# A gated mix of a long convolution and a mixer MLP: W1 products of one block ahead of the convolution taps, eight more steps and four evacuation engines changed, and ring slots given to the buffer that was free the longest

## The chip, the cores and the metric

The kernel runs on 1 core of one Trainium2 chip. The time is device microseconds of one execution. Three runs of the kernel before are at hand; one further execution was recorded by the hardware profiler, and all rows of a trace come from that one. A time within a row is counted from the first instruction of the span.

The engines are named as in the profile: PE is TensorE (PEld its weight loads), DVE is VectorE, ACT is ScalarE, POOL is GpSimd, and SP is the engine that issues most DMAs.

## The reference

S is 2048 tokens, D is 640, F is 1536, all inputs bf16. Cut to what matters (padding of the shifts and casts left out):

```python
g = sigmoid((q * gate_w).sum(-1, keepdims=True))

kv = short_conv(k, shift_k) * v                  # 4 taps along the tokens
y  = causal_long_conv(kv, ssm_k) + kv * ssm_D    # by rfft2/irfft2 of length 4096
a  = q * y

h  = gelu(layernorm(q) @ w1)                     # D x D
hs = shifted(h) @ w2                             # four groups of columns, shifted by +1, -1, +2, -2 tokens
x1 = q + hs
b  = x1 + gelu(layernorm(x1) @ w3) @ w4          # D x F, F x D

out = g * a + (1 - g) * b
```

## The kernel before, in words

Partition p holds 16 consecutive tokens (index t), so the sequence is handled in four blocks (0 to 3) of 4 x 128 tokens. All matrix products run on PE into eight PSUM banks; ACT and DVE empty the banks; SP starts the DMAs.

The work around the change is this:

- `k_load(c)` (L556) loads a block of k and turns it with PE (`transposed`, L610: 20 transposes into three PSUM banks `pst`), and copies each bank into `KT`. The letters of the step name say which engine empties which bank (`evac`, L358: ACT on L360, DVE on L362).
- `x_stats`, `x_norm`, `x_turn` give the layer norm of a block of q (held in `X`) and turn the result `xn` into `xt`. For blocks 0 and 1 the turn is made by PE and three copies; for blocks 2 and 3 (`D`) it is one DMA transpose that SP issues (L652).
- `mlp1(c, u)` (L700) makes the W1 products of block c, group u (five matmuls into a bank `psm1`, L707), and in a second step the GELU of that bank on ACT (L710) into `HT`.
- `tap(k, ev)` (L577) makes the four-tap convolution for 128 channels with matmuls of 32 x 128 (L590) into four banks `psk`, and multiplies with v: for an A the bank is first copied to `yk` on ACT (L599) and then multiplied on DVE (L602), for a V it is multiplied on DVE straight from the bank (L605).
- `t2_table` (L306) makes a table of twiddle factors in two halves: DVE makes integers `ab` (L266), POOL adds them into a grid `n` (L321), DVE masks it (L275), and ACT takes the sine. Its step 3 adds 2048 to `ab` for the second half.
- `step1` (L410) is the first stage of the transforms: matmuls into banks `ps1` (L423), and casts into `stg`, whose engine is given by a letter for each bank. `w2` (L777) makes the W2 products (L788), which DVE adds to X (L791).
- `w3` (L840) makes the W3 products and the GELU (L844) into ring buffers `gt`, and `w4` (L867) multiplies those with W4. `step4` (from L893) makes the last stage of the inverse transform and gates the result.

The order of all work is written out: `ORDER` holds 1099 step names of the form `step.arguments:k`, and the loop at the end calls the k-th piece of each step in that order, under a manual schedule. Each engine's queue is therefore exactly what the steps give it in that order, and an engine waits in order. The buffers of seven rings are also written out: `SLOTS` (L66) has one digit for each allocation of a tag, and `slot` (L81) takes them one after the other. Tag `c` are the eight PSUM banks, `row` four buffers of 4 x 640 values (k, xn, stg, q), `gt` four buffers shared by `n`, `ab` and the GELU results, and the others are smaller rings. A buffer is written only when those who read its earlier tenant are done.

```python
def slot(pl, shape, dt, name, tag, bufs):
    if tag not in SLOTS:
        return pl.tile(shape, dt, name=name, tag=tag, bufs=bufs)
    taken[tag] = taken.get(tag, -1) + 1
    return pl.tile(shape, dt, name=name, tag=tag + SLOTS[tag][taken[tag]], bufs=1)
```

Of the kernel before, what the change touches and what calls it, by code (L numbers as in the profile page):

```python
# [41 lines left out]
def kernel(  # L42
# [24 lines left out]
        "c": "012345670124703510347205142356401723605162370514731057423671045261304732641374153670421350627413"  # L67
             "502634751264351270361427503164257364102546173045621537426107432715604371401362570164301257613045"
             "267236057416537621507362651374026372401534762501373150427102547535706432073125640736450750634127"
             "504763270415367204325170635147630125460327156034215760147362304167135620316425031672301402715320"  # L70
             "1724107361761423564023714053627501267420674256271306234",
        "row": "01230213021302320123012031203120310310303",
        "gt": "012301031010231012301201",
# [805 lines left out]
    def step4(t1, ev):  # L879
# [32 lines left out]
        "open.L1.left:0 "  # L912
        "open.A2.right:0 "
        "consts0:0 "
        "load_x0.0:0 "
        "warm:0 "
        "load_x0.1:0 "
        "consts0:1 "
        "warm:1 "
        "warm:2 "  # L920
        "pow0:0 "
        "kv_alloc:0 "
        "k_load.3.AVA:0 "
        "f4_table:0 "
        "x_stats.0.VVVA:0 "
        "warm:3 "
        "k_load.3.AVA:1 "
        "x_stats.0.VVVA:1 "
        "load_x.1:0 "
        "x_stats.0.VVVA:2 "  # L930
        "k_load.3.AVA:5 "
        "x_stats.0.VVVA:3 "
        "x_stats.0.VVVA:4 "
        "x_stats.0.VVVA:5 "
        "x_stats.0.VVVA:6 "
        "warm:4 "
        "row_order:0 "
        "k_load.2.VAV:0 "
        "f1_table:0 "
        "x_norm.0.VVAA:0 "  # L940
        "x_norm.0.VVAA:1 "
        "f4_table:1 "
        "x_stats.1.VVVV:0 "
        "k_load.3.AVA:2 "
        "load_x.3:0 "
        "x_norm.0.VVAA:2 "
        "x_stats.1.VVVV:1 "
        "k_load.3.AVA:3 "
        "x_turn.0.AAA:0 "
        "k_load.3.AVA:6 "  # L950
        "k_load.2.VAV:5 "
        "load_w1.1:0 "
        "x_norm.0.VVAA:3 "
        "k_load.2.VAV:1 "
        "x_stats.1.VVVV:2 "
        "x_turn.0.AAA:1 "
        "x_stats.1.VVVV:3 "
        "x_turn.0.AAA:2 "
        "x_stats.1.VVVV:4 "
        "load_w1.0:0 "  # L960
        "x_stats.1.VVVV:5 "
        "x_stats.3.VVAA:0 "
        "k_load.3.AVA:4 "
        "x_norm.1.VVVV:0 "
        "x_turn.0.AAA:4 "
        "k_load.2.VAV:3 "
        "x_turn.0.AAA:3 "
        "x_turn.0.AAA:5 "
        "x_stats.3.VVAA:1 "
        "x_norm.1.VVVV:1 "  # L970
        "x_norm.1.VVVV:2 "
        "v_load.2:0 "
        "k_load.0.AAV:0 "
        "f1_table:1 "
        "mlp1.0.2:0 "
        "mlp1.0.3:0 "
        "x_norm.1.VVVV:3 "
        "v_load.0:0 "
        "k_load.1.AVV:0 "
        "k_load.2.VAV:6 "  # L980
        "mlp1.0.0:0 "
        "load_x.2:0 "
        "x_stats.3.VVAA:2 "
        "x_turn.1.VVV:0 "
        "x_turn.1.VVV:4 "
        "mlp1.0.1:0 "
        "x_stats.3.VVAA:3 "
        "x_turn.1.VVV:1 "
        "k_load.2.VAV:4 "
        "x_stats.3.VVAA:4 "  # L990
        "x_stats.3.VVAA:5 "
        "k_load.0.AAV:3 "
        "x_turn.1.VVV:5 "
        "mlp1.0.3:1 "
        "x_stats.3.VVAA:6 "
        "x_turn.1.VVV:2 "
        "v_load.3:0 "
        "x_turn.1.VVV:3 "
        "k_load.1.AVV:3 "
        "w1_mixed:0 "  # L1000
        "v_load.1:0 "
        "mlp1.0.0:1 "
        "x_stats.2.VVAA:0 "
        "mlp1.0.2:1 "
        "k_load.0.AAV:1 "
        "mlp1.0.1:1 "
        "x_stats.3.VVAA:7 "
        "k_load.0.AAV:5 "
        "mlp1.1.2:0 "
        "x_norm.3.VVVV:0 "  # L1010
        "x_norm.3.VVVV:1 "
        "k_load.0.AAV:4 "
        "load_cj:0 "
        "k_load.0.AAV:2 "
        "mlp1.1.2:1 "
        "x_norm.3.VVVV:2 "
        "x_norm.3.VVVV:3 "
        "x_stats.2.VVAA:1 "
        "k_load.1.AVV:5 "
        "mlp1.0.4:0 "  # L1020
        "k_load.1.AVV:4 "
        "mlp1.0.4:1 "
        "k_load.1.AVV:1 "
        "d_fold:0 "
        "mlp1.1.4:0 "
        "x_turn.3.D:0 "
        "kv_consts:0 "
        "x_stats.2.VVAA:2 "
        "mlp1.1.0:0 "
        "k_load.2.VAV:2 "  # L1030
        "k_wrap:0 "
        "k_load.1.AVV:6 "
        "mlp1.1.4:1 "
        "k_load.0.AAV:6 "
# [7 lines left out]
        "x_stats.2.VVAA:4 "  # L1042
        "h_shift.1:0 "
        "mlp1.1.3:1 "
        "tap.4.VAAV:0 "
        "x_stats.2.VVAA:5 "
        "tap.3.VAVA:1 "
        "tap.3.VAVA:3 "
        "tap.3.VAVA:5 "
        "h_shift.0:0 "  # L1050
# [1014 lines left out]
```

## Time and profile before

| what | us |
|---|---|
| the runs | 227.49, 231.56, 227.55 |
| median | 227.55 |
| the profiled execution | 227.13 |
| its span, first to last instruction | 225.4 |

The granted TensorE clock is 1.00 in the profiled execution. The difference between 227.13 and 225.4 lies around the span and is no part of any row.

How to read the rows that are shown further on. The line by stretch gives the stretch, its length, the busy time of PE, PEld, DVE, ACT and POOL with the number of instructions in brackets, then the granted clock, the busy share of the DMA engines and GB/s. A row of the chain of waits gives start, length and what ran. A row of the timeline gives start, length, engine, line, operation, output and inputs with shapes and how many were merged (x5); in square brackets stands how long the engine sat idle before it and what released it. A merged row's time to the next row's start is what the engine spent on it; its own length runs to the end of the last instruction, and matmuls overlap. Rows name tiles without their numbers.

### The profile page before, as it was taken

To read this page: it belongs to the slowest core of one execution; us is meant where nothing else is said; L and a number is where in the kernel's file an instruction comes from. 1 tells how busy PE (TensorE), PEld (TensorE's weight loads), DVE (VectorE), ACT (ScalarE), POOL (GpSimd) and SP (SyncE) were. 2 spreads that over 40 slices of the span, in tenths; PEclk is the share of its full clock that TensorE was granted. 3 is DMA by queue.
4 is the path that set the end of the run, shared out by engine and by line. 5 is a ranking of instruction groups with operands and counts; after the bars stand their busy time and mean duration, and the time that the engine had idled before them with its cause. 6 is when DMAs were issued, how large, how long until landed. Compare 5 with 4: busy or idle time off the path is not lost.

```text
span 225.4 us, 6053 instructions
## 1 busy us (share of the span) xinstructions
PE 217.8 (97%) x2427; PEld 121.5 (54%) x2428; DVE 183.7 (81%) x447; ACT 171.4 (76%) x341; POOL 38.1 (17%) x91
## 2 busy tenths in 40 slices
PE   8989999899999999999999999999999999999994
PEld 2557455447846563345664444556533547657762
DVE  7898998868889969963899988989999841439994
ACT  4899988787999999999987597967988450266450
POOL 4247246816000431300600000000000000000000
PEclk9999999999999999999999999999999999999999
DMA  6999998892998999999989570690794879429914
GB/s 226 374 376 344 258 280 170 317 364 107 361 365 355 348 295 265 410 334 343 254 219 338 116 243 0 191 379 17 119 305 166 249 259 366 175 60 305 324 70 179
DMA packets 41770, 57.61 MB, mean 256 GB/s; under 512 B 18446, under 2 KB 34446, under 8 KB 41486
## 3 DMA queue, kind: packets, MB, share of 16 engines
q1 hardware_dynamic: 41166, 54.60, 75.4%
q0 software_dynamic: 576, 2.62, 3.1%
q8 instruction: 19, 0.31, 0.6%
q14 instruction: 9, 0.07, 0.1%
HBM read 34.93 MB, written 18.35 MB: 236 GB/s over the span
## 4 chain that ended last, share of the span: by engine, by line
PE 79%; DMA 9%; DVE 4%; ACT 4%; issue 1%; POOL 1%; SPq 0%; ACTq 0%
PE ps L840 24%; PE ps L867 23%; PE psw L788 7%; PE ps L465 5%; PE ps L893 4%; DMA X<-in_A_q_dram 4%; PE psm L707 4%; DMA xt<-xn 3%; PE psz L228 3%; PE ps L512 3%; PE ps L423 2%; PE pst L390 2%; DVE X L791 2%; ACT stg L360 2%; DMA S_x<-stg 2%; PE psk L590 1%
## 5 line engine op out<-in xcount | busy, mean ns | idle before, releaser
L840 PE MATMUL ps<-x1t,W 128*128 128x512 bf16 x240 | 56.1, 380 | 0.1
L867 PE MATMUL ps<-W,gt 128*128 128x320 bf16 (+2 forms) x383 | 55.1, 299 | 0.1
L867 PEld LDWEIGHTS <-gt 128*128 128x128 bf16 x384 | 36.2, 98 | 17.7 <-issue 3.0
L844 ACT ACTIVATE gt<-ps 128x512 bf16<-128x512 f32 x48 | 27.6, 609 | 19.0 <-PE ps L867 10.6
L840 PEld LDWEIGHTS <-W 128*128 128x128 bf16 x240 | 21.9, 98 | 28.7 <-issue 5.9
L360 ACT CAST stg<-ps 128x512 bf16<-128x512 f32 x55 | 28.6, 604 | 2.3 <-PE ps L423 2.0
L870 DVE SCALAR_TENSOR_TENSOR X<-ps,OMG,X 128x320 bf16<-128x320 f32 (+2 forms) x32 | 17.2, 547 | 11.9 <-PE ps L867 11.7
L707 PE MATMUL psm<-xt,WA 128*128 128x512 bf16 x100 | 23.4, 379 | 1.9 <-DMA WA<-in_B_w_dram 0.8
L360 ACT CAST gs<-ps 128x320 bf16<-128x320 f32 x41 | 15.6, 440 | 8.8 <-PE ps L512 4.8
L788 PE MATMUL psw<-WA,HT 128*128 128x320 bf16 x116 | 21.4, 300 | 0.0
L362 DVE CAST XS<-ps 128x512 bf16<-128x512 f32 x19 | 12.5, 684 | 6.7 <-PE ps L465 6.7
L362 DVE CAST stg<-ps 128x512 bf16<-128x512 f32 x25 | 15.8, 683 | 1.9 <-PE ps L423 1.9
L707 PEld LDWEIGHTS <-WA 128*128 128x128 bf16 x100 | 9.2, 97 | 12.9 <-DMA WA<-in_B_w_dram 1.0
L360 ACT CAST hs<-ps 128x512 bf16<-128x512 f32 x28 | 15.0, 605 | 1.4 <-PE ps L465 1.4
L791 DVE SCALAR_TENSOR_TENSOR X<-psw,X 128x320 bf16<-128x320 f32 x32 | 14.5, 487 | 1.6 <-PE psw L788 1.6
L897 ACT ACTIVATE y<-ps,GS 128x320 bf16<-128x320 f32 x22 | 10.4, 526 | 5.7 <-PE ps L893 3.5
L710 ACT ACTIVATE HT<-psm 128x512 bf16<-128x512 f32 x20 | 11.8, 617 | 3.6 <-PE psm L707 3.5
L788 PEld LDWEIGHTS <-HT 128*128 128x128 bf16 x116 | 10.7, 98 | 6.8 <-issue 3.1
L362 DVE CAST gs<-ps 128x320 bf16<-128x320 f32 x23 | 10.7, 484 | 2.4 <-PE ps L512 1.7
L797 ACT ACTIVATE jk<-X 128x640 bf16<-128x640 bf16 x16 | 12.2, 761 | 0.5 <-DVE X L791 0.4
L788 PE MATMUL psw<-WA,HM 128*128 128x320 bf16 x44 | 12.3, 299 | 0.0
L360 ACT CAST XS<-ps 128x512 bf16<-128x512 f32 x21 | 11.8, 607 | 0.5 <-PE ps L465 0.3
(151 smaller groups left out, 346.6 us busy)
## 6 DMA issues: line engine op xcount, KB each, us to landing
S_x<-stg SPq DMA_DIRECT2D x8, 640.0 KB, 4.3
S_h<-stg SPq DMA_DIRECT2D x8, 640.0 KB, 4.8
ax<-S_x SPq DMA_DIRECT2D x8, 640.0 KB, 5.9
ax<-S_h SPq DMA_DIRECT2D x8, 640.0 KB, 8.1
S_g<-gs SPq DMA_DIRECT2D x8, 640.0 KB, 3.6
W<-in_B_w_dram SPq DMA_DIRECT2D x2, 1920.0 KB, 9.1
kn<-in_A_k_dram SPq DMA_DIRECT2D x4, 640.0 KB, 6.9
E<-in_A_ssm_k_dram SPq DMA_DIRECT2D x5, 512.0 KB, 6.1
```

Source lines behind the costliest of these rows:

```text
L360: A.copy(out=dst, in_=src)
L362: V.tensor_copy(out=dst, in_=src)
L465: PE.matmul(ps[j][q:q + 32, lo - 512 * u:hi - 512 * u], lhsT=CMP[HALF[j], 8 * b + 4 * h + i, c, :], rhs=st[name, 2 * b + h][HALF[j], i, lo ...
L707: PE.matmul(ps[:].rearrange("p (a b) -> p a b", a=4), lhsT=W1N[:, k, 160 * u:160 * u + P] if u < 4 else W1M[:, k, :], rhs=xt[:, :, k, :], ...
L710: A.activation(out=st["HT"][:, 4 * c:4 * c + 4, u, :], in_=ps[:].rearrange("p (t b) -> p t b", t=4), func=ACT.Gelu_apprx_tanh)
L788: PE.matmul(ps[:], lhsT=h_tile(f, t1), rhs=W2P[:, f, o:o + W], start=(f == 0), stop=(f == 4))
L791: V.scalar_tensor_tensor(out=X1[:, t1, o:o + W], in0=box["ps"][:], scalar=1.0, in1=X[:, t1, o:o + W], op0=ALU.mult, op1=ALU.add, accum_out ...
L797: A.activation(out=jk[:], in_=X1[:, t1, :], func=ACT.Square, accum_out=S12[:, 1, t1:t1 + 1])
L840: PE.matmul(ps[:].rearrange("p (a b) -> p a b", a=4), lhsT=st["W3"][:, k, f * P:(f + 1) * P], rhs=xt[:, :, k, :], start=(k == 0), stop=(k ...
L844: A.activation(out=st["gt", c, f // 4][:, f % 4, :], in_=ps[:], func=ACT.Gelu_apprx_tanh)
L867: PE.matmul(ps[:], lhsT=st["gt", c, f // 4][:, f % 4, i * P:(i + 1) * P], rhs=st["W4"][:, f, o:o + w], start=(f == 0), stop=(f == FC - 1))
L870: V.scalar_tensor_tensor(out=X1[:, t1, o:o + w], in0=box["ps"][:], scalar=OMG[:, t1:t1 + 1], in1=X1[:, t1, o:o + w], op0=ALU.mult, op1=ALU ...
```

## The change

The set of steps is the same. Of the 1099 steps these stand elsewhere (place before, place after): `mlp1.1.1:0`, the W1 products of block 1 and group 1, 139 to 127, and its GELU `mlp1.1.1:1` 147 to 135; `k_load.1:2` (the transposes of the second bank) 127 to 112; `load_w2:0` 125 to 138; `tap.3:0` 128 to 133 and `tap.4:0` 133 to 140; `t2_table:3` 443 to 320; `w2.14:3` 447 to 449; `step4.10:2` and `step4.8:6` change places near the end (1078, 1077).

Four evacuations change their engine: the first bank of `k_load.0` (into KT) from ACT to DVE; the third bank of `x_turn.1` (into xt) from DVE to ACT; one bank of `step1.KV.3` and one of `step1.HT0.1` (into stg) from ACT to DVE.

The digits of the rings `c` and `gt` are others. For `c` most of it gives the same sequence of tenants under other numbers. In `gt`, the last half differs in four places.

The diff, cut to its core (the list `ORDER` is also written with several steps to a line, which changes nothing):

```diff
     SLOTS = {
-        "c": "012345670124703510347205142356401723605162370514731057423671045261304732641374153670421350627413"
...
+        "c": "012345670124703513043725174501674235064513206457025460372105436712450347102340263145072365174023"
...
-        "gt": "012301031010231012301201",
+        "gt": "012301031012031201301201",
...
-        "x_stats.2.VVAA:3 "
-        "t2_table:0 "
-        "load_w2:0 "
-        "mlp1.1.3:0 "
-        "k_load.1.AVV:2 "
-        "tap.3.VAVA:0 "
-        "mlp1.1.0:1 "
...
+        "x_stats.2.VVAA:3 t2_table:0 mlp1.1.3:0 mlp1.1.1:0 mlp1.1.0:1 x_stats.2.VVAA:4 h_shift.1:0 mlp1.1.3:1 "
+        "x_stats.2.VVAA:5 tap.3.VAVA:0 tap.3.VAVA:1 mlp1.1.1:1 tap.3.VAVA:3 tap.3.VAVA:5 load_w2:0 h_shift.0:0 "
```

The first place is PE's queue at the end of the W1 products of block 1. `psm1` is a bank of W1 products, `psk` one of the taps. Before:

```order
L707 MATMUL psm1_539<-xt_385,WA_103 128x512
L590 LDWEIGHTS KT_155
L590 MATMUL psk_546<-DG_506,KT_155 128x128
L590 LDWEIGHTS KT_155
L590 MATMUL psk_547<-DG_506,KT_155 128x128
```

And after:

```order
L707 MATMUL psm1_538<-xt_385,WA_103 128x512
L707 LDWEIGHTS WA_103
L707 MATMUL psm1_544<-xt_385,WA_103 128x512
L707 LDWEIGHTS WA_103
L707 MATMUL psm1_544<-xt_385,WA_103 128x512
L707 LDWEIGHTS WA_103
L707 MATMUL psm1_544<-xt_385,WA_103 128x512
L707 LDWEIGHTS WA_103
L707 MATMUL psm1_544<-xt_385,WA_103 128x512
L707 LDWEIGHTS WA_103
L707 MATMUL psm1_544<-xt_385,WA_103 128x512
L590 LDWEIGHTS KT_155
```

The five matmuls of group 1 (psm1_544; before it was psm1_716, behind two taps) now stand ahead of the first tap.

The second place is DVE's queue at the normalisation of block 3 (xn_461), whose end lets SP issue the first DMA transpose. Before:

```order
L664 TENSOR_SCALAR xn_461<-X_102,RS_91,NB_92 128x640 x4
L362 COPY KT_155<-pst_419 128x1024
L552 TENSOR_REDUCE i32_507<-IDB_75 128x32
L553 TENSOR_TENSOR DG_506<-i32_507,cr_465 128x640
L362 COPY KT_155<-pst_269 128x1024
```

And after:

```order
L664 TENSOR_SCALAR xn_461<-X_102,RS_91,NB_92 128x640 x2
L362 COPY KT_155<-pst_438 128x1024
L664 TENSOR_SCALAR xn_461<-X_102,RS_91,NB_92 128x640 x2
L362 COPY KT_155<-pst_419 128x1024
L552 TENSOR_REDUCE i32_508<-IDB_75 128x32
```

The copy of pst_438 stands between the second and the third piece of the normalisation; it was ACT's before.

The third place is DVE's queue at the second half of the twiddle table (ab, n), between the additions of W2 products to X. Before:

```order
L791 SCALAR_TENSOR_TENSOR X_102,S12_82<-psw2_1692,X_102 128x320
L266 TENSOR_SCALAR ab_534<-ab_534 128x32
L275 TENSOR_SCALAR n_1753<-n_1753 128x1024
L341 TENSOR_SCALAR n_1756<-m_1532 128x512
L275 TENSOR_SCALAR n_1756<-n_1756 128x512
L791 SCALAR_TENSOR_TENSOR X_102,S12_82<-psw2_1743,X_102 128x320
```

And after:

```order
L791 SCALAR_TENSOR_TENSOR X_102,S12_82<-psw2_1693,X_102 128x320
L362 CAST stg_1727<-ps1_1721 128x4x128
L275 TENSOR_SCALAR n_1753<-n_1753 128x1024
L341 TENSOR_SCALAR n_1756<-m_1533 128x512
L275 TENSOR_SCALAR n_1756<-n_1756 128x512
L791 SCALAR_TENSOR_TENSOR X_102,S12_82<-psw2_1730,X_102 128x320
```

The addition to ab has left this place for one 123 steps earlier, and a cast of a bank of step 1 stands where it was.

More of the change, by code (lines that the diff above doesn't have):

```diff
@@ L911 @@
     ORDER = (
[L912 to L1034, printed above, removed]
-        "x_stats.2.VVAA:3 "
-        "t2_table:0 "
-        "load_w2:0 "
-        "mlp1.1.3:0 "
-        "k_load.1.AVV:2 "
-        "tap.3.VAVA:0 "
-        "mlp1.1.0:1 "
[L1042 to L1050, printed above, removed]
-        "mlp1.1.1:0 "
@@ L1382 @@
-        "step1.HT0.0.VAAVVAVAVV:4 "
-        "step1.HT0.0.VAAVVAVAVV:6 "
-        "step1.HT0.0.VAAVVAVAVV:1 "
-        "w3.0.9:1 "
-        "swap.L1.L2.left:0 "
-        "step1.HT0.0.VAAVVAVAVV:5 "
-        "step1.HT0.1.VVAAAAAAVA:1 "
-        "w3.0.6:0 "
-        "step1.HT0.1.VVAAAAAAVA:2 "
-        "w2.4:4 "
-        "step1.HT0.0.VAAVVAVAVV:12 "
-        "w3.0.6:1 "
-        "step1.HT0.0.VAAVVAVAVV:7 "
-        "step1.HT0.0.VAAVVAVAVV:8 "
-        "w3.0.7:0 "
-        "step1.HT0.0.VAAVVAVAVV:9 "
@@ L2008 @@
-        "store.8:1 "
-        "close.L2:0 "
-        "close.C:0 "
[169 rows of a table added]
     ).split()
```

948 lines of the change are left out of this document (4 added, 944 removed), and 167 rows, old and new, of the table ORDER.

## The prediction

> **What bounds the kernel now.** I read the page's busy shares first, then the busy time by stretch.
>
> ```profile
> span 225.4 us, 6053 instructions
> PE 217.8 (97%) x2427; PEld 121.5 (54%) x2428; DVE 183.7 (81%) x447; ACT 171.4 (76%) x341; POOL 38.1 (17%) x91
> ```
> ```profile
> 10.00:20.00 10.00, 8.47 (x91) 5.77 (x89) 9.69 (x33) 9.94 (x18) 4.45 (x6) 1.00 1.06 364
> 40.00:50.00 10.00, 9.25 (x124) 3.86 (x108) 7.99 (x15) 7.59 (x16) 5.32 (x9) 1.00 0.90 349
> 90.00:220.00 130.00, 129.94 (x1433) 70.82 (x1434) 103.31 (x196) 92.48 (x195) 5.90 (x18) 1.00 0.72 228
> ```
>
> The first figure behind the length is PE's busy time. From 90 to 220 PE is busy for 129.94 of 130.00 us, so there a delay of another engine matters only if it outlasts PE's cover, and what PE does is unchanged. PE loses time before 20 us, 0.75 in 40 to 50, and a little in 80 to 90. The end is therefore set by the last moment at which PE waits for something outside itself. The chain of waits names it.
>
> ```profile
> 24.32 7.63 DMA xt<-xn
> 39.69 1.12 PE psk L590 x76
> 40.83 0.59 ACT yk L599
> 41.46 2.33 PE psm L707 x10
> ```
> ```profile
> 41.46 1.89 PE L707 MATMUL psm<-xt,WA 128*128 128x512 bf16 x8 [0.75 <-ACT yk L599]
> ```
> ```profile
> 39.14 0.58 ACT L599 CAST yk<-psk 128x512 bf16<-128x512 f32 x1
> ```
> ```profile
> 24.32 4.08 SPq L652 DMA_TRANSPOSE xt<-xn  x1
> 34.74 3.73 SPq L652 DMA_TRANSPOSE xt<-xn  x1
> ```
> ```profile
> DMA to landing us min/median/max: 6.6/7.1/7.6
> ```
>
> PE's 0.75 us before 41.46 is put down to a cast of yk, but the bank that these W1 products of block 2 take was read by the earlier cast, which ended at 39.14 + 0.58 = 39.72. The other input is block 2's turned x: the second DMA transpose is issued at 34.74, and with the shorter landing time of 6.6 it is there at 41.34. I take that transpose as the wait that ends last. Behind 41.46 PE has no wait until 85. So the time goes with the second transpose's issue, less what PE gets back later.
>
> **Term 1: the KT copy on VectorE, +0.61.** The copy of the first bank of k_load.0 goes from ACT to DVE, between the second and third normalisation of x block 3.
>
> ```profile
> 21.78 0.89 DVE L685 BATCH_NORM_STATS2 b<-X 128x6 f32<-128x320 bf16 x2 [0.53 <-DMA X<-in_A_q_dram]
> ...
> 22.82 1.47 DVE L664 TENSOR_SCALAR xn<-X,RS,NB 128x640 bf16<-128x640 bf16 x4
> 24.21 0.68 DVE L362 COPY KT<-pst 128x1024 bf16<-128x1024 bf16 x1
> 24.82 0.36 DVE L552 TENSOR_REDUCE i<-IDB 128x32 bf16<-128x128 bf16 x1
> ...
> 33.81 0.87 DVE L664 TENSOR_SCALAR xn<-X,RS,NB 128x640 bf16<-128x640 bf16 x2
> ```
>
> The price stands in the next row of the same shape: from 24.21 to the next start at 24.82 it takes 0.61 of DVE (0.68 by its length). DVE waits 0.53 for X before 21.78; from there to 34.68, the end of block 2's last normalisation, the timeline shows it no other wait, and the second transpose goes out at 34.74. So +0.61 at 24.3 moves the first transpose to about 24.93 and the second to 35.35. The bounds are 0 (the landing doesn't follow the issue) and +0.68; I take 0.61, the distance of starts. The other changed evacuation here, one xt copy of block 1, leaves DVE for ACT.
>
> ```profile
> L360 ACT COPY xt<-pst x3: 611/1006/1027, 12.0 to 13.8; 128x1024 bf16<-128x1024 bf16 x2, 128x512 bf16<-128x512 bf16 x1
> L362 DVE COPY xt<-pst x3: 412/636/692, 18.6 to 20.3; 128x1024 bf16<-128x1024 bf16 x2, 128x512 bf16<-128x512 bf16 x1
> ```
>
> The 0.41 that DVE saves lies ahead of its 0.53 wait for X, which covers it: nothing is gained. ACT's 0.61 delays the first GELUs, and is made good where ACT later has one KT copy less:
>
> ```profile
> 21.84 1.96 ACT L360 COPY KT<-pst 128x1024 bf16<-128x1024 bf16 x2
> ```
>
> Half of this row, 0.98, leaves ACT. If that cover failed, ACT would be late for yk by at most 0.61, which is within the first term's own bound.
>
> **W1 products of block 1 ahead of the taps, 0.**
>
> ```profile
> 30.54 1.24 PE L707 MATMUL psm<-xt,WA 128*128 128x512 bf16 x5
> 32.00 3.41 PE L707 MATMUL psm<-xt,WA 128*128 128x512 bf16 x15 [0.23 <-DMA xt<-xn]
> ```
>
> PE spends its 1.24 earlier and the taps start later by about 1.14. Their results go to casts on ACT and multiplications on DVE, where DVE is itself 0.61 later. Ahead of 32.00 PE waited 0.23 for the first transpose. PE has the same work to do before that wait and reaches it at the same time, while the transpose lands 0.61 later: about 0.85 of waiting, and up to 0.23 + 0.61 + 1.24 = 2.1 if the taps had slack that the moved products now fill. It costs nothing as long as the second transpose is what PE waits for next: PE has the 0.75 in hand at 41.46, grown by the same 0.61. The fourth bank of the second tap waits for the moved GELU a few tenths; that is in the same cover. The move of k_load.1:2 and load_w2 leaves the sequence of SP and of POOL as it was: 0.
>
> **Term 2: the table's addition 62 us earlier, −0.66.** t2_table:3 adds 2048 to ab on DVE, and POOL makes n from it.
>
> ```profile
> 81.09 0.18 DVE L266 TENSOR_SCALAR ab<-ab 128x32 int32<-128x32 int32 x1
> 83.29 0.69 DVE L275 TENSOR_SCALAR n<-n 128x1024 int32<-128x1024 int32 x1 [2.02 <-POOL n L321]
> ...
> 85.92 0.69 DVE L362 CAST stg<-ps 128x512 bf16<-128x512 f32 x1
> 86.53 0.48 DVE L791 SCALAR_TENSOR_TENSOR X<-psw,X 128x320 bf16<-128x320 f32 x1
> ```
> ```profile
> 81.35 1.91 POOL L321 TENSOR_TENSOR n<-ab 128x1024 int32<-128x1024 int32 x1 [4.85 <-DVE ab L266]
> ```
> ```profile
> 80.96 0.82 PE L423 MATMUL ps<-HT,F 64*128 64x512 bf16 x6
> ...
> 84.99 0.30 PE L788 MATMUL psw<-WA,HM 128*128 128x320 bf16 x1
> 85.24 0.70 PE L788 MATMUL psw<-WA,HT 128*128 128x320 bf16 x4
> ...
> 86.01 1.02 PE L423 MATMUL ps<-HT,F 64*128 64x512 bf16 x4
> 87.07 1.24 PE L840 MATMUL ps<-x1t,W 128*128 128x512 bf16 x5
> ```
>
> DVE waits 2.02 for POOL, POOL had waited 4.85 for DVE. With ab ready long before, POOL, idle from 81.35 − 4.85 = 76.5, runs n from there and is done by 78.4. The 2.02 goes, but DVE now has a stg cast there (0.69, the first of the block's stage-1 banks that ACT took before). It needs PE's bank, so DVE starts it at about 81.9 and is some 0.8 earlier than before at 83.3. Behind that the banks of W2 and stage 1 come free 0.8 earlier, and PE's late starts vanish: 0.11 at 85.24 (0.25 from start to start where 0.14 is usual), and in the four L423 that take 1.06 from 86.01 to the next start, where six from 80.96 to 81.72 take 0.76: four would take 0.51, so 0.55. Sum 0.66. The bounds are 0 (another wait takes their place) and −0.7. I take the full value, since 0.8 exceeds the largest of the two.
>
> **The rest, 0.** The cast of step1.KV.3 that goes to DVE lies in 43 to 50, where PE shows no wait. The swap in step 4 and w2.14:3 move past one or two neighbours; the store behind the swap isn't the last one. Renumbered PSUM banks are nearly all the same order of reuse. The new ring for gt gives one wait:
>
> ```profile
> 126.53 0.60 ACT L844 ACTIVATE gt<-ps 128x512 bf16<-128x512 f32 x1 [0.78 <-PE ps L867]
> 127.02 0.42 ACT L360 CAST gs<-ps 128x320 bf16<-128x320 f32 x1
> 128.69 0.60 ACT L844 ACTIVATE gt<-ps 128x512 bf16<-128x512 f32 x1 [1.25 <-PE ps L840]
> ```
> ```profile
> 125.78 1.79 PE L867 MATMUL ps<-W,gt 128*128 128x320 bf16 x12
> ...
> 129.67 0.48 PE L512 MATMUL ps<-hs,INV 32*64 32x320 bf16 x16
> ```
>
> The GELU at 126.53 must now wait until W4's products have read their gt, at 125.78 + 1.79 = 127.57: +1.04 for it and for the cast queued behind it. Both are done before 128.69, where ACT had waited 1.25, and PE asks for these banks from 129.67 on: 0.
>
> **The sum.** The profiled execution took 227.13 with a span of 225.4. 225.4 + 0.61 − 0.66 = 225.35, or about 227.1 for that execution. The median shown, 227.55, stands 0.42 above it, so I name 227.55 − 0.05 = 227.5.
>
> **The rivals.**
> A, the transposes are not what is delayed. The first took 7.63 from issue to landing and the second 6.6, so the DMA load may set the landing rather than the issue. Then term 1 is 0 and 227.55 − 0.66 = 226.9. Against it: the first transpose landed in a stretch full of loads; at the second there are fewer.
> B, the PE waits at 85 to 87 stay: the stg cast, which needs PE, takes the place of POOL. Then 227.55 + 0.61 = 228.15. For it: 0.8 is not much more than 0.55; against it: 2.02 of waiting go, and only 0.69 of work comes.
> C, the wait of 1.04 on ACT reaches PE: 227.5 + 1.04 = 228.5. It decides if the work behind 126.53 passes 129.67; that work is done by about 127.57 + 0.60 + 0.42 = 128.6, so 1.1 us are left.
> D, slower through the clock: PE's wait ahead of block 3's products grows so long that TensorE slows down.
>
> ```profile
> 0.98 7.35 PE L228 MATMUL psz<-WZ 128*128 128x512 bf16 x20 [0.98 <-DVE NPI L248]
> ```
>
> At the start 20 products took 7.35, against 20 × 3.41/15 = 4.55 at the pace of the row of 32.00: 2.8 lost, hence 227.5 + 2.8 = 230.3. Against it: from 10 to 20 us PE is idle for 1.53 and its granted clock is 1.00, and the wait that I expect is 0.85 to 2.1. The Trainium skill, "TensorE: Matmul & The Clock Gate", Part 1 (the HAM clock gate), says the rate halves after about 3.4 us of idleness and returns after as much work; by that rule D does not happen here, and no row of this trace shows an idle stretch that long behind the start.
>
> **How the numbers follow.** My forecast 0.45, A 0.2, B 0.2, C 0.05, D 0.05, and 0.05 for things not listed. The range takes in A with the profiled execution's 0.42 below the median (226.9 − 0.4 = 226.5, I say 226.4) and C's 228.5 with the larger length of term 1: 226.4 to 228.7. Only D and the unlisted lie outside, and the spread of single runs. 2% is 4.55 us, about what a measurement of this kernel can tell from no change: faster needs under 223.0, for which no case speaks (0.02); slower needs over 232.1, D with a second mishap (0.04); within it 0.94.
>
> **What would show it.** Right: the transposes are issued at about 24.9 and 35.3, PE starts block 2's products at about 42.1, POOL's n runs near 76.5, DVE has no 2 us wait near 83, the four L423 near 86 take half a microsecond, and PE's later work stands within 0.1 of where it stood. A: PE restarts at 41.5. B: the late starts at 85 to 87 are still there. C: PE waits between 129 and 131. D: a clock below 1.00 in 30 to 40 us. It would also be wrong if PE waited again behind 42 for banks that ACT or DVE free late.

## The result, and the profile after

| | before | after |
|---|---|---|
| the runs | 227.49, 231.56, 227.55, 227.81 | 232.09, 231.81, 230.86, 231.23 |
| median | 227.68 | 231.52 |
| the profiled execution | 227.13 | 232.09 |
| its span | 225.4 | 230.3 |

The ratio after to before is 1.0154, with an interval of 1.0112 to 1.0196: the changed kernel is slower by 1.5%, 231.5 where 227.5 was predicted, and outside the range of 226.4 to 228.7. A ratio takes in only the runs within 1.5% of the fastest of their kernel.

The same two views of after that the prediction opens with: the page's busy line, and the busy time by stretch.

```profile
span 230.3 us, 6053 instructions
PE 217.0 (94%) x2428; PEld 121.0 (53%) x2428; DVE 186.8 (81%) x449; ACT 170.6 (74%) x339; POOL 37.7 (16%) x91
```
```profile
10.00:20.00 10.00, 8.49 (x91) 5.79 (x89) 9.66 (x33) 9.95 (x19) 4.31 (x5) 1.00 1.05 370
30.00:40.00 10.00, 6.66 (x254) 4.19 (x244) 6.24 (x20) 5.95 (x11) 5.23 (x15) 1.00 1.02 189
40.00:50.00 10.00, 8.75 (x146) 3.88 (x133) 8.84 (x15) 7.04 (x13) 6.61 (x14) 1.00 0.80 279
90.00:130.00 40.00, 39.22 (x471) 19.13 (x469) 31.66 (x64) 35.66 (x74) 6.56 (x21) 1.00 0.98 300
130.00:220.00 90.00, 89.99 (x954) 49.85 (x952) 71.06 (x133) 58.39 (x123) 0.00 (x0) 1.00 0.66 205
```

And one stretch of before that the prediction did not need:

```profile
30.00:40.00 10.00, 9.65 (x250) 5.40 (x242) 9.14 (x24) 8.33 (x17) 6.78 (x19) 1.00 0.88 208
```

PE does the same work. It is idle for 3.3 us in 30 to 40, where before it was idle for 0.35, and from 130 on nothing differs. To see where 4.9 us of span went, I take from the timelines of PE when each stage's first (or last) matmul starts. The last two columns are a second pair of profiles, of the same two kernels run on one chip (experiments 5 and 6).

| stage | before | after | before again | after again |
|---|---|---|---|---|
| start to the first stage-1 matmul on KV | 43.71 | 46.03 | 44.76 | 46.30 |
| from there to the first W2 product | 7.12 | 8.51 | 7.10 | 7.45 |
| W2 products, first to last | 34.95 | 35.77 | 34.83 | 36.11 |
| from there to the first W4 product | 19.16 | 19.61 | 19.68 | 19.62 |
| W4 to the end of the last matmul | 117.05 | 117.04 | 117.05 | 117.05 |

So the first pair loses 2.32 + 1.39 + 0.82 + 0.45 = 4.98, the second 1.54 + 0.35 + 1.28 − 0.06 = 3.11. Three places carry it.

**The first place: PE stands for its own instructions.** PE's timeline of after, from the end of the first two taps:

```profile
31.31 1.47 PE L707 MATMUL psm<-xt,WA 128*128 128x512 bf16 x6
34.97 2.10 PE L707 MATMUL psm<-xt,WA 128*128 128x512 bf16 x9 [2.19 <-issue]
...
38.26 0.39 PE L590 MATMUL psk<-DG,KT 32*128 32x128 bf16 x15
39.80 0.58 PE L590 MATMUL psk<-DG,KT 32*128 32x128 bf16 x33 [1.15 <-issue]
...
43.59 2.50 PE L707 MATMUL psm<-xt,WA 128*128 128x512 bf16 x10
```

"Issue" means that PE waited for nothing that the profile shows. Both waits fall inside a run of equal matmuls, so no operand is late. Counted from 0 over PE's records (4856 matmuls and weight loads and 14 others, 4870 in all), they stand ahead of number 705 and number 961, which is 256 apart. The page lists a queue of instruction transfers with 19 packets, about one for each 256 of the 4870. One answer on the DMA queues of after for 32.3 to 33.5 has one of these packets, and there is none from 29.5 to 32.3:

```profile
q8 instruction: 1, 0.02, 5.0%
```

In before the same piece comes in 29.7 to 30.9:

```profile
q8 instruction: 1, 0.02, 5.1%
```

In before it runs from 29.78 to 30.76, and PE passes number 705 at 33.31 without a wait. In after it runs from 32.40 to 33.36, and PE, whose last record ahead of number 705 starts at 32.40, goes on at 34.97, 1.6 behind the end of the transfer. The second transfer runs from 37.00 to 38.28, and PE goes on at 39.80, 1.5 behind its end.

The Trainium skill, "Runtime: NRT & Kernel Launch", section "Instruction fetch mechanics", says that engines refill their instruction memory in blocks of 16 KiB, 256 instructions, and that the cost of crossing such a boundary is "mostly hidden". The spacing of 256 agrees with the traces; hidden it is not where PE comes early to the edge through short matmuls: in after PE stands 2.19 and 1.15.

The consequence for the prediction's chain: SP's timeline of after.

```profile
24.52 3.95 SPq L652 DMA_TRANSPOSE xt<-xn  x1
...
34.47 4.31 SPq L652 DMA_TRANSPOSE xt<-xn  x1
```

With 7.1 to landing the second transpose is there at 41.6, and PE comes to block 2's products only at 43.59, without a wait for it.

**The second place: POOL's addition holds up a multiplication.** DVE and POOL in after, and then the same last multiplication in before:

```profile
45.61 2.00 DVE L602 TENSOR_TENSOR KV<-yk,KV 128x512 bf16<-128x512 bf16 x1
```
```profile
45.41 1.91 POOL L321 TENSOR_TENSOR n<-ab 128x1024 int32<-128x1024 int32 x1
```
```profile
47.66 0.61 PE L423 MATMUL ps<-KV,F 64*128 64x512 bf16 x4 [1.24 <-DVE KV L602]
```
```profile
42.89 0.64 DVE L602 TENSOR_TENSOR KV<-yk,KV 128x512 bf16<-128x512 bf16 x1
```

The multiplication takes 2.00 instead of 0.64 and ends at 47.61, just behind POOL's addition (45.41 + 1.91 = 47.32). PE waits 1.24 for it.

**The third place: the other addition meets the normalisations, and a store lands late.** DVE and POOL of after, PE's six stage-1 matmuls that follow, and DVE's cast of step1.HT0.1:

```profile
80.39 3.07 DVE L664 TENSOR_SCALAR xn<-X,rn 128x640 bf16<-128x640 bf16 x4
...
86.90 0.69 DVE L362 CAST stg<-ps 128x512 bf16<-128x512 f32 x1 [0.59 <-DMA S_h<-stg]
87.51 0.68 DVE L275 TENSOR_SCALAR n<-n 128x1024 int32<-128x1024 int32 x1
```
```profile
80.31 1.91 POOL L321 TENSOR_TENSOR n<-ab 128x1024 int32<-128x1024 int32 x1
```
```profile
84.81 1.52 PE L423 MATMUL ps<-HT,F 64*128 64x512 bf16 x6
...
90.54 0.71 PE L423 MATMUL ps<-HT,F 64*128 64x512 bf16 x4
```

And the normalisations in before:

```profile
76.55 1.51 DVE L664 TENSOR_SCALAR xn<-X,rn 128x640 bf16<-128x640 bf16 x4
```

DVE's wait of 2.02 is gone, as predicted, and the four matmuls near 86 (now at 90.54) take 0.74 to the next start instead of 1.06. But the four normalisations take 1.56 longer, and the six matmuls behind them take 1.56 from start to start instead of 0.76: their banks come free late. The cast that moved to DVE waits 0.59 for the landing of an earlier store of the buffer it writes.

The rest of the loss is one wait for a weight load, which experiment 5 shows in before as well (0.44):

```profile
109.92 5.06 PE L867 MATMUL ps<-W,gt 128*128 128x320 bf16 x36 [0.69 <-DMA W<-in_B_w_dram]
```

### The profile page after: what moved, and what is told of

Read it like the earlier page. It is cut to its first block, busy times and chain, and to the rows that moved or that the text cites. A ratio compares the mean times of both kernels' runs of the same rounds, so it can differ in the third digit from the quotient of the medians.

```text
span 230.3 us, 6053 instructions
## 1 busy us (share of the span) xinstructions
PE 217.0 (94%) x2428; PEld 121.0 (53%) x2428; DVE 186.8 (81%) x449; ACT 170.6 (74%) x339; POOL 37.7 (16%) x91
## 4 chain that ended last, share of the span: by engine, by line
PE 75%; DMA 10%; ACT 6%; DVE 5%; issue 2%; SPq 0%; DVEq 0%
PE ps L867 23%; PE ps L840 19%; PE psm L707 7%; PE psw L788 6%; DMA W<-in_B_w_dram 5%; PE ps L893 4%; PE ps L465 4%; PE ps L423 3%; DMA kn<-in_A_k_dram 3%; PE ps L512 3%; DMA S_h<-stg 2%; PE psk L590 2%; PE pst L390 2%; ACT stg L360 1%; DVE X L791 1%
## 5 line engine op out<-in xcount | busy, mean ns | idle before, releaser
L360 ACT CAST stg<-ps 128x512 bf16<-128x512 f32 x53 | 27.7, 604 | 4.2 <-PE ps L423 4.0
L362 DVE CAST stg<-ps 128x512 bf16<-128x512 f32 x27 | 17.1, 681 | 1.9 <-PE ps L423 1.1
```

The lines of the kernel that those rows point to most:

```text
L360: A.copy(out=dst, in_=src)
L362: V.tensor_copy(out=dst, in_=src)
```

## The experiments

Every ratio is to runs of before on the same chip. Before took 228.8 to 229.7 there, not 227.7. Its first profile had no wait at number 705, while experiment 5 has one; of the 1.4 us between these two profiles 1.05 lie ahead of KV. In the expectations F is the theory that PE's instruction transfers cost the time, H that it is the bank of step1.HT0.1 given to DVE, and N that the engine of that cast makes no difference and the loss of that stretch lies elsewhere, as in POOL's addition into n. "Edge" is a place in PE's stream 256 instructions from the last. "KV" is the first stage-1 matmul on KV, as in the table above.

**1. The products of block 1 alone.** Before, with the moved products, their GELU and after's digits of ring c.

```diff
+ mlp1.1.3:0 mlp1.1.1:0 ... tap.3.VAVA:1 mlp1.1.1:1 tap.3.VAVA:3
- tap.3.VAVA:5 h_shift.0:0 mlp1.1.1:0 tap.4.VAAV:7 ... z_cols:0 mlp1.1.1:1 load_gw:0
```


> The kernel before with one move alone: W1 products of block 1, group 1 ahead of the two taps (and the PSUM bank numbers that go with it). Theory F (PE's instruction fetch): the pages of 256 PE instructions are fetched by a DMA of 16 KB; with the products ahead, PE crosses the page edge 1.1 us later, the fetch falls behind the load of W2, and PE stands still without instructions. Then this move alone makes the whole loss: 230.5 to 232, with a stall of about 2 us in the middle of the W1 products of block 3 that no semaphore explains, and the fetch at about 32.4 instead of 29.8. Theory T (the engine changes delay DVE or ACT, and PE waits for them): this kernel has none of them and takes 227.5, plus or minus 0.5.

Ratio 0.9986 (0.9943 to 1.0028). KV at 44.63, in before again 44.76. The move alone costs nothing measurable, though PE waits 1.26 at number 705, so F's price was wrong. Its ten runs spread wider than before's, though, from 228.17 to 235.94, and three of them, at 233.93 to 235.94, have a granted clock of 0.990 to 0.993.

**2. All but the products.** After, with the products and their GELU back behind the taps and before's digits of ring c.

```diff
- mlp1.1.3:0 mlp1.1.1:0 mlp1.1.0:1
+ h_shift.0:0 mlp1.1.1:0 tap.4.VAAV:7
```


> The kernel after, with the W1 products of block 1, group 1 put back behind the two taps (PSUM bank numbers of before); all other edits stay. Theory F: the fetch is at about 29.8 again, no stall, 226.5 to 228. Theory T: the loss stays, 230.5 to 232.

Ratio 0.9997 (0.9959 to 1.0036). The second transpose is issued at 36.21, in before again at 35.75: +0.46. PE starts block 2 at 42.90 instead of 42.50. F wanted the transfer back at 29.8 and no wait, and T wanted the loss to stay; the transfer begins at 32.62, PE waits 1.21 at number 705, and the loss is gone, so neither holds as it was put. The normalisations take 3.07, and the W2 stage 35.53.

**3. The edges moved.** After, with seven warm-up matmuls split in four, which puts 42 more instructions ahead of all others.

```diff
+ if n == 11 and i < 7:
+     for q in range(4):
+         PE.matmul(ps[:, q * P:q * P + P], lhsT=WZ[:], rhs=WZ[:], start=True, stop=True)
+     continue
```


> The kernel after, with seven of the first warm-up matmuls each split into four of a quarter of the width: 42 more PE instructions at the start, about the same work, nothing else changed. They move every later page edge 42 instructions ahead in the program, so that PE crosses the second edge at about 27 instead of 29.5, before the load of W2 is issued. Theory F: the stall of 2.19 goes and the time falls by 2 to 4 us to 227.5 to 229.5, although work was added. Theory T: no change, 231.5 plus or minus 0.7.

Ratio 1.0132 (1.0066 to 1.0197). The waits stay at numbers of the same spacing, 705 and 1217, and so stand at other matmuls, inside taps (0.94 and 1.34 of idle PE). They belong to the count of instructions, not to a place of the program. The time stays, where F wanted 2 to 4 us less.

**4. W2's load behind the second transpose**, so that fewer transfers run when PE asks for its instructions.

```diff
- tap.3.VAVA:5 load_w2:0 h_shift.0:0
+ x_turn.2.D:0 load_w2:0
```


> The kernel after, with the two loads of W2 (0.8 MB) put behind the second DMA transpose in SP's queue. Theory F with the data loads as what delays the fetch: the second fetch starts within about 1.5 us of the page edge (about 31 instead of 32.4), and the stall of 2.19 shrinks to under 1 us; the third fetch may now be late instead, since the loads come at 38.6; 228 to 231.5. Fetch late for another reason (the DMA transpose): the fetch stays 2.9 us behind the edge, and the stall stays. Theory T: no change of PE's wait.

Ratio 1.0143 (1.0086 to 1.0199). The transfer starts 1.86 behind the edge (30.02, 31.88) instead of 2.89, and PE waits 0.96 instead of 2.19. But PE then waits 1.15 for the second transpose at 42.6, and 1.53 for a late load at 53.15. The wait is shorter, the time is not. In experiments 3 and 4 the second place is there as well (8.65 and 8.84 from KV to W2), so they don't give the price of the first alone.

**5 and 6. The two kernels again, unchanged**, each with ten runs.

> The kernel before, unchanged, as a yardstick with a trace of its own beside the others. Theory F (PE's instruction fetch ends the wait wherever the taps stand close): the time is the same as before by its meaning; where a run takes about 2 us more than the 227.5 seen first, its trace shows a stall of 1.5 to 2 us at PE instruction 705, the page edge, and where it takes 227.5 it shows none. Theory V (the spread of times comes from something else, such as the data loads): a run that takes longer shows no stall at a page edge.

> The kernel after, unchanged, beside the kernel before on the same chip. Theory F: again stalls at PE instructions 705 and 961, and 1 to 2% slower than before. Theory V: about as slow as either half of the change alone, within 0.5% of before, and the first comparison was one of two chips or moments.

Ratios 1.0000 (0.9962 to 1.0038) and 1.0057 (1.0021 to 1.0093): the loss is there again, but smaller. Before's PE rows:

```profile
34.68 2.10 PE L707 MATMUL psm<-xt,WA 128*128 128x512 bf16 x9 [1.11 <-issue]
```
```profile
42.50 1.67 PE L707 MATMUL psm<-xt,WA 128*128 128x512 bf16 x7 [0.49 <-DMA xt<-xn]
```

So the wait at number 705 is no effect of the change, and behind it PE still waits 0.49 for the second transpose, the prediction's chain. In after the wait is longer, and the clock falls behind it:

```profile
35.18 2.96 PE L707 MATMUL psm<-xt,WA 128*128 128x512 bf16 x9 [1.96 <-issue]
```
```profile
36.00:40.00 4.00, 4.00 (x106) 2.45 (x107) 1.76 (x4) 1.22 (x3) 1.75 (x6) 0.57 0.94 147
```

The granted clock is 0.57 from 36 to 40, and the nine products take 2.96 instead of 2.10. From the end of the wait to block 2's products (44.03) PE needs 8.85, in before again 7.33 without its last wait of 0.49: the clock takes 1.5 us of this profile. In the first profile of after it stayed 1.00 there, though PE had waited 2.19. The Trainium skill, "TensorE: Matmul & The Clock Gate", Part 1, names about 3.4 us of idleness for this; here it fell behind a wait of 1.96, so the page alone did not exclude rival D.

**7. The table's addition alone.** Before, with t2_table:3 moved ahead.

```diff
+ h_shift.2:2 t2_table:3
- step1.HT0.1.VVAAAAAAVA:4 t2_table:3
```


> The kernel before with one move alone: the table's addition (t2_table:3) 123 steps earlier. By the prediction's second term: 0.66 less, as DVE's 2.02 wait for POOL goes, and PE's late starts at 85 to 87 with it. Theory P (POOL's two-input addition over 128 x 1024 holds DVE up while it runs, as the trace of after has it at 80.3, where four normalisations took 3.07 instead of 1.51): nothing gained, 0 plus or minus 0.4, since the addition now runs beside the normalisation.

Ratio 1.0014 (0.9976 to 1.0053), where term 2 wants 0.997. DVE's and PE's rows:

```profile
77.65 3.06 DVE L664 TENSOR_SCALAR xn<-X,rn 128x640 bf16<-128x640 bf16 x4
```
```profile
82.06 1.51 PE L423 MATMUL ps<-HT,F 64*128 64x512 bf16 x6
...
87.78 0.60 PE L423 MATMUL ps<-HT,F 64*128 64x512 bf16 x4
```

The four matmuls at 87.78 take 0.54, so the 0.55 that the prediction named is back. The six at 82.06 take 1.55 to the next start at 83.61, against 0.76 in before: 0.79 is lost. The profile shows the meeting; the ratio's interval, −0.5 to +1.2 us, only just leaves out term 2's −0.66.

**8. After without the table's move.**

```diff
- h_shift.2:2 t2_table:3
+ step1.HT0.1.VVVAAAAAVA:4 t2_table:3
```


> The kernel after with the table's addition back at its place of before; all else as after. By the second term: 0.66 more than after. Theory P: as after, plus or minus 0.4; the normalisation takes 1.5 again, and DVE's 2 us wait for POOL is back. Theory F: the stalls at PE instructions 705 and 961 are as in after, since they lie 40 us ahead of this edit.

Ratio 1.0127 (1.0053 to 1.0201), wide, and no faster than after. Its profiled execution took 237.36, where its other runs took 231.06 to 233.42, and is left aside. Inconclusive.

**9, 10 and 12. The edges moved far, by 170 instructions.** After, before, and the kernel of experiment 11, each with 85 small matmuls of 32 x 32 behind the first warm-up loop.

```diff
+ for i in range(85 if n == 11 else 0):
+     PE.matmul(ps[:, 0:32], lhsT=WZ[0:32], rhs=WZ[0:32, 0:32], start=True, stop=True)
```


> The kernel after with 85 tiny matmuls (32 rows, 32 columns) behind the first 11 warm-up matmuls, so 170 more PE instructions, while PE waits for k anyway. Every later page edge moves 170 instructions ahead in the program: the edges then fall at about 20.5 us, at the start of the second tap (30.5), in the third (36) and at the start of the fifth (40), and between them lie 5 us or more, except for the last. The 42 of the third run moved the edge only 0.4 us, within the tap. Theory F (PE's instruction fetch): the stalls of 2 to 2.6 us at 32 to 35 go, at most one of about 1 us is left near 40, and the time falls by 1 to 2.5 us against after (to 0.99 to 1.002 of before). Theory S (the taps wait for data, and instructions only seem to be the reason): no change against after, 1.005 to 1.015 of before.

> The kernel before with the same 85 tiny matmuls. Theory F: the stall of 1.5 us at PE instruction 705 that the kernel before showed in its second trace goes, and PE then waits for the second DMA transpose instead, which takes back a part: 0.990 to 0.998 of before. Theory S: 1.000 to 1.004.

> The kernel after with both: the 85 tiny matmuls, and the cast of step1.HT0.1 on ACT. If F and H both hold, their gains add: 0.985 to 0.998 of before. If only F holds, the time is that of the run with the tiny matmuls alone.

Ratios 1.0153 (1.0109 to 1.0196), 1.0111 (1.0066 to 1.0156) and 1.0110 (1.0069 to 1.0151). All are slower than F wanted; 9 lies at the end of S's range and 10 above it. The long wait of 32 to 36 is gone in all three. In 9 PE then waits 0.72 at a later edge, 0.44, 0.68 and 1.41 for KV, which is the second place again; in 12 it waits 1.45 at the later edge. In 10, on before, it waits for the second transpose:

```profile
43.87 1.46 PE L709 MATMUL psm<-xt,WA 128*128 128x512 bf16 x6 [2.17 <-DMA xt<-xn]
```

Part of that is the price of the tool: the small matmuls take 2.29, and the first tap starts 0.3 and 0.7 later (30.06 and 29.18) than in experiments 6 and 5 (29.75 and 28.49). So these runs don't give the price of the waits; they show that PE, once free of them, stands behind DVE and the transposes.

**11. The bank of step1.HT0.1 back to ACT**, otherwise after.

```diff
- step1.HT0.1.VVVAAAAAVA
+ step1.HT0.1.VVAAAAAAVA
```


> The kernel after with one bank of step1.HT0.1 cast by ACT again, as before. Theory H (DVE, which now holds this cast, waits for the landing of the S_h store that frees its buffer, with the additions to X queued behind it, and PE waits for their banks): the wait of 0.6 to 1.3 on DVE near 86.5 goes, PE's stage from 75 to 96 gets 0.3 to 1.0 shorter, and the time falls by as much. Theory N (the wait only changes its engine): no change against after, plus or minus 0.4.

Ratio 1.0039 (1.0008 to 1.0070), which does not part from after's 1.0057. The wait for the store moves to ACT with the cast:

```profile
87.51 1.07 ACT L360 CAST stg<-ps 128x512 bf16<-128x512 f32 x2 [1.17 <-DMA S_h<-stg]
```

H falls: the store is late, whoever writes the buffer next.

**13. POOL's first addition later**, beside casts from PSUM instead of multiplications; otherwise after.

```diff
+        yield
         ts(ab[:, NG:], R64[:, 0:32], col(23))
...
+ tap.1.VAVA:4 t2_table:9
```


> The kernel after, with the last of DVE's small operations on ab (the one that lets POOL start its first addition) put behind the last multiplication with KV, so that POOL's addition runs beside DVE's casts from PSUM only. Theory P (POOL's two-input addition slows DVE's operations on SBUF, and this meets KV's last multiplication): the last multiplication takes 0.4 to 0.6 again, the time from the first stage-1 matmul to the first of W2 is 7.1 to 7.5 us (8.5 in after), and the time falls by 0.3 to 1.4 us. Theory F (only the page edges cost): no change against after, plus or minus 0.4.

Ratio 1.0089 (1.0051 to 1.0127). The second place is cured: from KV (44.72) to the first W2 product 7.24, and DVE's casts beside the addition keep their pace:

```profile
45.31 3.26 DVE L363 CAST stg<-ps 128x512 bf16<-128x512 f32 x5
```
```profile
45.92 1.91 POOL L322 TENSOR_TENSOR n<-ab 128x1024 int32<-128x1024 int32 x1 [0.57 <-DVE ab L266]
```

But the time did not fall as P wanted: the W2 stage takes 36.52, with this wait on DVE:

```profile
85.39 0.69 DVE L363 CAST stg<-ps 128x512 bf16<-128x512 f32 x1 [1.62 <-DMA S_h<-stg]
```

**14. POOL's first addition earlier in before**, so that it meets the multiplications.

```diff
+            if c == 0:
+                yield
...
+ t2_table:8 h_shift.3:2
```


> The kernel before, with POOL's first addition for the table ahead of the last masks (h_shift.3:2) in POOL's queue, so that it runs about 1.8 us earlier and meets the last multiplications with KV. Theory P: one of these takes about 2 us instead of 0.4 to 0.6, the time from the first stage-1 matmul to the first of W2 grows from 7.1 to 8 to 8.6, and the time grows by 0.5 to 1.4 us (1.002 to 1.006 of before). Else no change, plus or minus 0.4.

Ratio 1.0065 (1.0036 to 1.0093).

```profile
43.18 2.53 DVE L604 TENSOR_TENSOR KV<-yk,KV 128x512 bf16<-128x512 bf16 x2
```
```profile
43.35 2.08 POOL L321 TENSOR_TENSOR n<-ab 128x1024 int32<-128x1024 int32 x1
```

Two multiplications take 2.53, in before again 0.86, and from KV to W2 it is 9.00 instead of 7.10. The meeting alone makes before slower by 0.65%: 1.5 us of 228.8, with an interval of 0.8 to 2.1.

**15 and 16. Fewer warm-up matmuls and the 85 small ones**, in after and in the kernel of experiment 13.

```diff
-        for n in (11, 3, 3, 3, 3):
+        for n in (5, 3, 3, 3, 3):
...
+            for i in range(85 if n == 5 else 0):
```


> The kernel after with the 85 tiny matmuls, but with 6 of the first 11 warm-up matmuls left out in exchange, so that PE is ready for k as early as before (158 more PE instructions). Theory F: no stall above 1 us at a page edge from 30 to 36; 1 to 2 us less than after, if PE's arrival is what sets the end there. Theory P alone: no change, as the taps end where DVE and the DMA transpose let them.

> The kernel after with both edits. If both theories hold, their gains add, 1.3 to 3 us less than after, which is as fast as before or faster (0.990 to 1.002). If only one holds, the time is that of its run alone.

Ratios 1.0181 (1.0150 to 1.0211) and 1.0151 (1.0108 to 1.0193), both misses. KV at 46.77 and 47.37: the shorter warm-up makes the first products start later (14.64 and 15.49, in before again 13.13), and in 16 the granted clock is 0.50 from 24.26 to 27.67. Nothing on the edges can be read from them.

**17. Term 2 without the meeting.** Before, with t2_table:3 moved ahead and POOL's second addition right behind it, which takes a buffer of ring gt earlier.

```diff
+            if c:
+                yield
...
+ h_shift.2:2 t2_table:3 t2_table:8
- "gt": "012301031010231012301201",
+ "gt": "012301031002013230123023",
```


> The kernel before with the table's addition 123 steps earlier and POOL's second addition right behind it (the mask on DVE stays; three ring slots of the table buffers changed with it), so that POOL is done at about 69 and meets no normalisation. Theory P: the four normalisations near 78 take 1.5 us, DVE's wait of 2.0 for POOL is gone, the late starts of PE at 86 to 88 (0.55 to 0.66) go without the 0.8 near 82, and the time falls by 0.3 to 0.7 us (0.997 to 0.9985 of before); the stage of W2 is 34.2 to 34.5 us long (34.8 to 34.95 before). Otherwise, if POOL now slows DVE's additions to X near 67 as much, no change.

Ratio 0.9975 (0.9954 to 0.9997): faster than before by 0.25%, 0.57 us of 228.97, the lowest ratio here, though its interval overlaps those of experiments 1 and 2.

```profile
64.61 1.91 POOL L321 TENSOR_TENSOR n<-ab 128x1024 int32<-128x1024 int32 x1 [10.17 <-PE ps L425]
```
```profile
77.72 1.51 DVE L666 TENSOR_SCALAR xn<-X,rn 128x640 bf16<-128x640 bf16 x4
```
```profile
82.13 0.82 PE L425 MATMUL ps<-HT,F 64*128 64x512 bf16 x6
...
87.07 0.61 PE L425 MATMUL ps<-HT,F 64*128 64x512 bf16 x4
```

The addition is over at 66.5, the normalisations take 1.51, the six matmuls 0.76 and the four 0.54: both stretches are free at once. The 0.57 lies near the 0.66 of term 2, with an interval of 0.1 to 1.1. The W2 stage is 34.74 long, not 34.2 to 34.5 as expected: the four matmuls stand behind its last product.

**18. After with the three repairs**: the first addition late, the second early, the bank on ACT.

```diff
+ tap.1.VAVA:4 t2_table:9 ... h_shift.2:2 t2_table:3 t2_table:8
- step1.HT0.1.VVVAAAAAVA
+ step1.HT0.1.VVAAAAAAVA
- "gt": "012301031012031201301201",
+ "gt": "012301031002013203103203",
```


> The kernel after with POOL's first addition behind the last multiplication with KV, its second at about 66 instead of 80, and the bank of step1.HT0.1 cast by ACT again; the products of W1 stay ahead of the taps, and the KT copy stays on DVE. If the three meetings are the whole loss: 0.995 to 1.003 of before, the stage of W2 34.2 to 34.7 us long (35.8 to 36.5 in after). If the page edges cost by themselves: 1.005 to 1.010.

Ratio 1.0049 (1.0013 to 1.0085): still slower than before. The normalisations take 1.51 and KV to W2 takes 7.27, but PE waits 1.93 at number 705, KV is at 45.49, and the W2 stage takes 36.35. Ahead of KV PE waits last for the second transpose, which SP issues at 36.34 (in before again at 35.75):

```profile
43.22 2.33 PE L710 MATMUL psm<-xt,WA 128*128 128x512 bf16 x10 [0.19 <-DMA xt<-xn]
```

In the W2 stage there is this:

```profile
87.21 0.70 PE L791 MATMUL psw<-WA,HT 128*128 128x320 bf16 x4 [1.19 <-ACT stg L363]
```

## Why the prediction was wrong

**The step that failed first: "W1 products of block 1 ahead of the taps, 0".** It rested on the words "it costs nothing as long as the second transpose is what PE waits for next". Alone that holds (experiment 1: 0.9986). In the changed kernel PE stood at two edges of its instruction stream and came to block 2's products at 43.59, two us behind the transpose. That PE stood there is shown, but a wait's length is not its price. Behind number 705 the same work is left, and PE goes on there at 34.97 and 35.18 in after, in before again at 34.68 behind its own wait of 1.11: 0.3 and 0.5 later (1.7 and 1.9 later than in the first profile of before, which had no wait there). The rest of the delay up to block 2 is the second wait (1.15) in the first profile of after and the lower clock (1.5) in the second. Why the waits are longer in after (2.19 and 1.96 against 1.11) is argued only: PE runs from number 449 to 705 in 2.9 us in after (29.51 to 32.40), in before again in 3.8, in the first profile of before in 4.9, while the transfer starts at about the same time in after and before again (32.40 and 32.16). With the products ahead PE is sooner at the edge, and waits. The rows of before put a busy PE there, and no row of it showed a wait of that kind, so the price had no row to come from.

**The step that failed in sign: "the table's addition 62 us earlier, −0.66".** What it named came true: DVE's 2.02 went, and in experiment 7 the four late matmuls were in time (0.54; in after they still take 0.74). What it left out stood in its own rows: POOL was to run n "from there", from 76.5, and at 76.55 DVE begins four normalisations. They cost 1.56 of DVE and 0.79 of PE (experiment 7), so by the rows the term alone is about +0.1 and not −0.66; with the meeting taken away the time falls by 0.57 (experiment 17). Rival B, in which the late starts at 85 to 87 stay, is not what happened; the bound of 0, "another wait takes their place", is, at a place that the prediction did not name.

**Not foreseen: the first addition against the multiplications.** No step moved POOL's first addition into them; everything ahead of KV came later on PE and DVE, while POOL did not come later by as much (its addition 43.92 before, 45.41 after; the last multiplication from 42.89 to 45.61). The stretch from KV to W2 lost 1.39 in the first pair of profiles and 0.35 in the second, where the addition began at 46.63, with the multiplications nearly done; experiment 14 shows that such a meeting costs about 1.5.

**Term 1, +0.61 on the transposes: near its size in other kernels, not in after.** In experiment 2 the second transpose is 0.46 later than in before again and PE 0.40; in experiment 18 they are 0.59 and 0.72 later, and PE ends on a wait for it. In after X landed in time, DVE had no wait where it had waited 0.53 before, and the transposes went out at 24.52 and 34.47 instead of the predicted 24.93 and 35.35. There it decided nothing, since PE was later still.

**The rest, 0: right behind 130.** From 130 to 220 PE is busy for 89.99 of 90, so the new ring of gt (five digits differ, not four) costs nothing, and rival C did not come. Of the new digits of c this is not shown: no run changes them alone.

**Rival D** had 0.05, with 2.8 us. It came in one of the two profiles of after, where it took about 1.5, and not in the one that belongs to the result. The mean granted clock of a run tells where else it came: 4 us at 0.57 leave about 0.993 of 230 us. At 0.993 or less stand 11 of the 50 runs in the ratios of after and its variants with the same warm-up and the products ahead (the result, 4, 6, 8, 11, 13 and 18), none of the 52 in 2, 5, 7, 14 and 17, where the products stand behind the taps, and 3 of the 98 of before beside them; of experiment 1, none of the six in its ratio and the three named there. So it seems to come with the moved products (the count was made afterwards, and no run tests it), but it is only a part of the loss: without its two such runs the median of experiment 6 is 230.2, still 0.4% over before's 229.3, and of the four runs of the result only one stands at 0.993.

**What stays open.** Neither half of the change costs anything measurable alone, and the whole 0.6 to 1.5%. Experiment 18 takes away both meetings and keeps 0.5%, of which three of its twelve runs, at a clock of 0.993 and 231.26 to 231.41, make a good part: the median of the other nine is 229.27, against 228.97 of before. Its profile is 0.73 later than experiment 5 at KV (term 1), loses 0.16 more up to W2 and 1.52 in the W2 stage, and gets 0.62 back ahead of W4. The wait at the edge has no price of its own from any run (9, 10, 12, 15 and 16 changed the warm-up as well). In after and in experiments 4, 6, 9, 11, 13 and 15 a store of step 1 lands late (0.59 to 1.62 of waiting), in the profiles of before it does not; I did not find its cause. Nor was the renumbering of the ring c tried alone: for 74 of its 439 digits the distance to the last use of the same bank is another.

## What to carry to other kernels

When a step is moved to free a waiting engine, look up what every other engine does at the time at which the freed one will now run: an operation of POOL that had been waiting may fall beside DVE work on SBUF and cost more than the wait did. A wait put down to nothing that the profile shows, at equal steps of the instruction count, belongs to the instruction stream; dense runs of short matmuls get there sooner. And two edits that are each free can cost together, so price the path with both in place, and look at the granted clock of every run, not of the profiled one alone.

## What the runs showed of the hardware

- While POOL adds two integer operands (128x1024, 1.91 us), DVE's work on SBUF nearly stands: a multiplication of two SBUF operands took 2.00 instead of 0.64, four normalisations 3.07 instead of 1.51, and both ended only behind POOL's end, at 47.61 and 83.46 against 47.32 and 82.22. Casts from PSUM beside it kept their pace (five in 3.26, experiment 13), and additions to X with one operand from PSUM their 0.49 (experiment 17). The Trainium skill, "GPSIMD Engine Reference", section 1, says that GpSimd shares its SBUF interface with VectorE, with contention for two SBUF inputs or a two-port mode; the traces agree for the multiplication, whose two operands lie in SBUF; whether the normalisations, which read one large operand, fall under the other case no trace shows. The price was 1.4 to 1.7 of POOL's 1.9 to 2.1 us.
- PE's instructions come in pieces of 256; from 10 to 60 us a transfer took 0.9 to 1.5 us (once 2.5) and mostly began 1.0 to 3.8 us behind PE's passing of the last edge, and where PE came to the next edge early it went on only 1.3 to 1.9 us behind the transfer's end. These waits were 0.5 to 2.2 us.
- In experiment 6 the granted clock was 0.57 from 36 to 40 us, behind a wait of 1.96 on PE; in the first profile of after it stayed 1.00 behind 2.19. In experiment 16 it was 0.50 from 24.26 to 27.67, behind waits of 0.96 and 0.84 on PE that ended at 22.33 and 24.24.
